# Queries and keys turned by VectorE in 32x32 blocks instead of by TensorE, with a fourth buffer for the activation tiles

## The chip, the cores and the metric

One core of one Trainium2 chip runs the whole program. The metric is the device time of one execution in microseconds, from the first to the last instruction and what the launch adds around them; smaller is better. TensorE, VectorE, ScalarE, GpSimd and SyncE run side by side, each in its own program order, and wait for one another by semaphores. SyncE issues every transfer of this kernel; sixteen DMA engines carry them out.

## The reference

Chunked attention with a few memory keys in front, then two feed-forward networks, all in float32:

```python
# q, k, v: 4 x 8 heads x 768 x 64; mem_k, mem_v: 4 x 8 x 8 x 64
for c in range(S // 32):                       # chunks of 32 queries
    l, r = max(0, 32 * c - 16), min(S, 32 * c + 32 + 8)
    k_full = concatenate([mem_k, k[:, :, l:r]], axis=2)
    v_full = concatenate([mem_v, v[:, :, l:r]], axis=2)
    a = softmax(q[:, :, 32 * c:32 * c + 32] @ k_full.T / 8)
    out[:, :, 32 * c:32 * c + 32] = a @ v_full
x = out as 3072 tokens x 512
x = (s * relu(x @ w_in) ** 2 + b) @ w_out      # 512 -> 2048 -> 512
x = (silu(x @ w_gate) * (x @ w_val)) @ w_out2  # 512 -> 1536 -> 512
```

## The kernel before

Attention is worked off in 24 groups of 128 queries (`GQ`), six to a batch, all eight heads at once. A group needs its queries and keys with the head dimension on the partitions, because TensorE contracts over partitions. `load_tokens` brings them in row by row (a token on each partition, 256-byte pieces, one for each head); `stage_queries` and `stage_keys` turn them on TensorE by products with the identity into the PSUM tiles `psQ` and `psK`, and `stage_queries_copy` and `stage_keys_copy` (lines L228 and L230) copy them to `qt` and `kt` in SBUF. `kt` holds for each of the group's four chunks the 8 memory keys and a window of 56 keys. Then come the scores (`psS`), the softmax, its turning (`psA`), the product with the values (`psV`) and the turning of the result (`psO`) into the tiles `xhi` and `xlo`. Where the values of one group and the scores of the next fall on one place, `stage_both` merges them in one block, `psB`.

The first network runs over 8 blocks of 384 tokens (three groups each) and 16 slices of its 2048 hidden columns. A step is twelve products into `hp` (the up product) and twelve into `acc` (the down product); between them ScalarE and VectorE make relu, square, bias and the split of the result into a rounded part `ghi` and a rest `glo`. `r` is the tile of this work, three buffers in the pool `gp`, and the copies `y` of finished blocks take their buffers from the same three. Weights come in raw as `raw_first` (1 MB for each slice) and are split into such pairs by ScalarE and VectorE (`split`, lines L774 to L838). The second network has three passes over the same tokens, with a scheme of seven products per block.

The order of all this is written by the class `Plan`: each piece of work is a task with an engine, a planned length, the tasks it depends on, and rings of buffers that it takes and gives. TensorE's order is that in which tasks are added; for the other engines and for SyncE's queue a list scheduler picks the next ready task by the longest way to the end. `START` is the order on TensorE at the beginning, when the first groups are worked off before and between the first steps; `VISITS` says at which half step of a block each stage of the later groups stands; `LOADS` fixes the order of the first transfers; `MOVED` names tasks that take the second of two possible engines. Groups 0 to 5 (`EARLY`) keep their queries and keys in slots of the weight pool, and only groups 6 to 23 use the tiles `q`, `ka` and `kb`.

```python
        t = plan.add(PE, 0.44, lambda: stage_queries(g, early), [qk], take=["acc2"] if early else ["a"])
```

Of the kernel before, what the change touches and what calls it, by code (L numbers as in the profile page):

```python
# [10 lines left out]
F32 = mybir.dt.float32  # L11
# [8 lines left out]
CHUNK, LEFT, RIGHT = 32, 16, 8  # L20
GQ = 128
# [6 lines left out]


START = (  # L30
    "Q0 T0 S0 Q1 T1 A0 V0 S1 Q2 A1 T2 X0 S2 V1 A2 X1 V2 X2 Q3 T3 U S3 Q4 U A3 D T4 U S4 D V3 "
    "U A4 X3 Q5 D V4 U T5 X4 D U S5 D A5 V5 X5 D U "
)

VISITS = {
# [6 lines left out]
}  # L42

LOADS = (
    "W0 K0 W2 K1 V0 W1 K2 V1 W4 V2 K3 W3 K4 V3 W6 W5 K5 V4 W9 W8 V5 W7 W10 "
)

MOVED = (
# [10 lines left out]
)  # L59


# [84 lines left out]
def attention_and_two_mlps(  # L146
# [52 lines left out]
    LENT = 3  # L199
    EARLY = 2 * GPB  # L200

    const = ctx.enter_context(tc.tile_pool(name="const", bufs=1))
    wp = ctx.enter_context(tc.tile_pool(name="wp", bufs=SLOTS))
    xp = ctx.enter_context(tc.tile_pool(name="xp", bufs=2))
    gp = ctx.enter_context(tc.tile_pool(name="gp", bufs=3))
    stp = ctx.enter_context(tc.tile_pool(name="stp", bufs=2))
    dram = ctx.enter_context(tc.tile_pool(name="dram", bufs=1, space=DRAM))
    ps_acc = ctx.enter_context(tc.tile_pool(name="ps_acc", bufs=1, space=PSUM))
# [17 lines left out]
    def copy(engine, out, in_):  # L226
        if engine == "ACT":
            nc.scalar.activation(out=out, in_=in_, func=AF.Copy)  # L228
        else:
            nc.vector.tensor_copy(out, in_)  # L230
# [58 lines left out]
    def load_tokens(g):  # L289

        b, gi = divmod(g, GB)
        s0 = gi * GQ
        if g < EARLY:
            t = wp.tile([P, 4, H * D], F32, tag="w", name=f"qk{g}")
            tq, ka, kb, sc = (t[:, i] for i in range(4))
        else:
            tq, ka, kb = (ld.tile([P, H * D], F32, tag=n, name=f"{n}{g}") for n in ("q", "ka", "kb"))
            sc = None
        every = slice(0, H)
        a, z = s0 - LEFT, s0 + GQ + RIGHT  # L300
        left, over, n = max(0, -a), max(0, z - S), HALF - NMEM
        rows(ka, mem_k, b, every, 0, NMEM)
        if left:
            rows(ka[NMEM:], k, b, every, 0, left)
        rows(ka[NMEM + left:], k, b, every, a + left, n - left)
        rows(tq, q, b, every, s0, GQ)
        rows(kb, k, b, every, a + n, HALF - over)
        if over:
            rows(kb[HALF - over:], k, b, every, S - over, over)
        loaded.setdefault(g, {}).update(q=tq, ka=ka, kb=kb, sc=sc)  # L310

    def load_values(g):

        b, gi = divmod(g, GB)
        s0 = gi * GQ
        n = g % 2
        if n not in v_bufs:
            v_bufs[n] = ld.tile([P, NC, NP, D], F32, tag=f"v{n}", name=f"v{n}")
        tv = v_bufs[n]
        for e in range(2):  # L320
            p0 = e * KC
            if gi < 2:
                mem = tv[p0:p0 + NMEM]
                nc.sync.dma_start(out=mem[:, 0], in_=mem_v[b, e:H:2].rearrange("h s d -> s h d"))
                for c in range(1, NC):
                    nc.gpsimd.tensor_copy(mem[:, c], mem[:, 0])
            for c in range(NC):
                a = s0 + c * CHUNK - LEFT
                left, over = max(0, -a), max(0, a + WIN - S)
                for row, first, n in (  # L330
                    (0, 0, left), (left, a + left, WIN - left - over), (WIN - over, S - over, over)
                ):
                    if n:
                        r0 = p0 + NMEM + row
                        nc.sync.dma_start(
                            out=tv[r0:r0 + n, c],
                            in_=v[b, e:H:2, first:first + n, :].rearrange("h s d -> s h d"),
                        )
        loaded.setdefault(g, {})["v"] = tv
# [65 lines left out]

    def scores_to(g):
        if "sc" not in staged[g]:
            sc = loaded[g]["sc"]
            if sc is None:
                sc = ap_.tile([P, H * KC], F32, tag="sc", name=f"sc{g}")  # L410
            staged[g]["sc"] = sc.rearrange("p (j e s) -> p j e s", j=NP, e=2)
        return staged[g]["sc"]
# [322 lines left out]
    def second_store(h, s, i):  # L735
# [7 lines left out]
    plan = Plan(  # L743
        dict(w=SLOTS - LENT, wt=SLOTS - 2, fly=2),
        dict(
            sc=LENT, f=2, own=1, qk=1, v=2, kt=1, qt=1, at=1, on=1, x=2, r=3, ghi=2, glo=2, acc01=1,
            acc2=1, acc3=1, a=2, h=2, yq=1, so=1, z=5, a1=1, a2=1, a3=1, v1=2, v2=1,
        ),
    )
# [3 lines left out]
    def either(name, lengths, emit, *args, **kwargs):  # L753

        engine = list(lengths)[name in moved]
        return plan.add(engine, lengths[engine], lambda: emit(engine), *args, **kwargs)

    issues = {}

    def transfer(deps, emit, n, kilobytes, get=(), take=(), give=(), rate=380.0, name=None):  # L760

        issue = issues[name] = plan.add(SP, 0.45 * n, emit, deps, [*get, "fly"], take=take)
        return plan.add(MOVE, kilobytes / rate, None, [issue], put=["fly"], lag=1.8, give=give)
# [97 lines left out]
    at_ = {}  # L861

    def plan_queries(g, early):
        qk = transfer(
            [], lambda: load_tokens(g), 4, 590, take=["sc"] if g < EARLY else ["qk"], rate=180.0, name=f"K{g}"
        )
        vv = transfer([], lambda: load_values(g), 8, 460, take=["v"], rate=180.0, name=f"V{g}")
        at_[g] = {"v": vv, "qk": qk}
        t = plan.add(PE, 0.44, lambda: stage_queries(g, early), [qk], take=["acc2"] if early else ["a"])
        at_[g]["qt"] = either(  # L870
            f"q{g}", {ACT: 0.50, DVE: 0.60}, lambda e: stage_queries_copy(e, g), [t], take=["qt"],
            give=["acc2"] if early else ["a"],
        )

    def plan_keys(g, early):
        t = plan.add(
            PE, 0.55, lambda: stage_keys(g, early), [at_[g]["qk"]], take=["acc01"] if early else ["a", "a"],
            give=[] if g < EARLY else ["qk"],
        )
        for i in range(2):  # L880
            t = either(
                f"k{g}_{i}", {ACT: 0.45, DVE: 0.54}, lambda e, i=i: stage_keys_copy(e, g, i, False), [t],
                take=["kt"] if i == 0 else (),
            )
            t = either(
                f"m{g}_{i}", {ACT: 0.26, DVE: 0.20}, lambda e, i=i: stage_keys_copy(e, g, i, True), [t],
                give=[] if early else ["a"],
            )
        if early:
            plan.rings["acc01"].append(t)  # L890
        at_[g]["t"] = at_[g]["qt"], t
# [66 lines left out]

    def plan_w1(m):
        if m not in split1:  # L960
            landed = transfer([], lambda: load_w1(m), 2, 1024, ["w", "w"], name=f"W{m}")
            split1[m] = split(landed, raw1, m, lambda: wp, f"first{m}", w1)

    def plan_up1(t, m):
# [287 lines left out]
```

## Time and profile before

| | us |
|---|---|
| median of three runs (1245.95 to 1248.83) | 1245.95 |
| the profiled execution, its own time | 1246.5 |
| its span, first to last instruction | 1244.7 |
| TensorE busy | 1204.2 |
| VectorE busy | 737.4 |
| ScalarE busy | 531.9 |
| GpSimd busy | 26.5 |

The busy times come from the page's first part. They are sums over the program, and the stages differ, so a change is read from the stretch in which it lies. The span is 1.8 us shorter than the execution's own time, which also has what lies around the first and last instruction.

### The profile page before, as it was taken

To read this page: it belongs to the slowest core of one execution; us is meant where nothing else is said; L and a number is where in the kernel's file an instruction comes from. 1 tells how busy PE (TensorE), PEld (TensorE's weight loads), DVE (VectorE), ACT (ScalarE), POOL (GpSimd) and SP (SyncE) were. 2 spreads that over 40 slices of the span, in tenths; PEclk is the share of its full clock that TensorE was granted. 3 is DMA by queue.
4 is the path that set the end of the run, shared out by engine and by line. 5 is a ranking of instruction groups with operands and counts; after the bars stand their busy time and mean duration, and the time that the engine had idled before them with its cause. 6 is when DMAs were issued, how large, how long until landed. Compare 5 with 4: busy or idle time off the path is not lost.

```text
span 1244.7 us, 25671 instructions
## 1 busy us (share of the span) xinstructions
PE 1204.2 (97%) x10512; PEld 1145.3 (92%) x10512; DVE 737.4 (59%) x1435; ACT 531.9 (43%) x1100; POOL 26.5 (2%) x54
## 2 busy tenths in 40 slices
PE   4788999999999999999999999999999999999998
PEld 3678999999999999999999999999999999999997
DVE  6889874444344343443579876668964448744444
ACT  4454532434333333333358554445543335433332
POOL 2011000000000000000000000000000000000000
PEclk9998999999999999999999999999999999999999
DMA  8864242212222122230273555567755558545532
GB/s 190 219 182 166 88 112 43 60 36 61 55 50 60 36 61 54 50 92 4 99 248 119 162 187 186 186 234 283 249 193 186 185 186 312 195 187 187 187 119 94
DMA packets 168014, 174.31 MB, mean 140 GB/s; under 512 B 108376, under 2 KB 139608, under 8 KB 166360
## 3 DMA queue, kind: packets, MB, share of 16 engines
q1 hardware_dynamic: 167896, 172.66, 43.2%
q8 instruction: 83, 1.36, 0.4%
q14 instruction: 35, 0.29, 0.1%
HBM read 124.65 MB, written 47.97 MB: 139 GB/s over the span
## 4 chain that ended last, share of the span: by engine, by line
PE 90%; DMA 4%; SPq 2%; DVE 2%; issue 1%; ACT 1%; POOL 0%; DVEq 0%; ACTq 0%; POOLq 0%
PE acc L494 7%; PE hp L494 7%; PE acc L495 7%; PE acc L496 7%; PE hp L496 7%; PE hp L495 7%; PE chain_a L494 5%; PE chain_a L495 5%; PE chain_a L496 5%; PE oacc L495 5%; PE oacc L494 5%; PE oacc L496 5%; PE chain_b L495 4%; PE chain_b L496 4%; PE chain_b L494 4%; DMA raw_first<-in_moe_w_out_dram 2%
## 5 line engine op out<-in xcount | busy, mean ns | idle before, releaser
L494 PE MATMUL acc<-ghi,w_first 128*128 128x384 f32 x512 | 177.7, 347 | 4.2 <-DVE ghi L547 3.9
L494 PE MATMUL hp<-xhi,w_first 128*128 128x384 f32 x512 | 176.5, 345 | 0.6 <-ACT xhi L228 0.6
L495 PE MATMUL acc<-glo,w_first 128*128 128x384 f32 x512 | 172.6, 337 | 0.2 <-DVE glo L556 0.2
L496 PE MATMUL acc<-ghi,w_first 128*128 128x384 f32 x512 | 172.6, 337 | 0.0
L495 PE MATMUL hp<-xlo,w_first 128*128 128x384 f32 x512 | 171.9, 336 | 0.4 <-DVE xlo L487 0.4
L496 PE MATMUL hp<-xhi,w_first 128*128 128x384 f32 x512 | 171.9, 336 | 0.0
L682 ACT ACTIVATE kept<-chain_a 128x256 f32<-128x256 f32 x216 | 82.9, 384 | 159.5 <-PE chain_a L496 131.9
L534 DVE SCALAR_TENSOR_TENSOR r<-r,s_sb 128x384 f32<-128x384 f32 x89 | 55.0, 618 | 145.8 <-ACT r L523 145.6
L523 ACT ACTIVATE r<-hp 128x384 f32<-128x384 f32 x107 | 52.7, 492 | 204.2 <-PE hp L496 204.1
L494 PE MATMUL oacc<-w_down,ghi 128*128 128x512 f32 x288 | 114.2, 396 | 0.1
L495 PE MATMUL oacc<-w_down,ghi 128*128 128x512 f32 x288 | 114.2, 397 | 0.0
L496 PE MATMUL oacc<-w_down,glo 128*128 128x512 f32 x288 | 112.2, 389 | 0.0
L494 PEld LDWEIGHTS acc<-ghi,w_first 128*128 128x128 f32 x512 | 96.8, 189 | 6.1 <-issue 4.2
L494 PEld LDWEIGHTS hp<-xhi,w_first 128*128 128x128 f32 x512 | 96.6, 189 | 2.4 <-ACT xhi L228 0.9
L495 PEld LDWEIGHTS acc<-glo,w_first 128*128 128x128 f32 x512 | 96.8, 189 | 0.8 <-DVE glo L556 0.8
L495 PEld LDWEIGHTS hp<-xlo,w_first 128*128 128x128 f32 x512 | 96.7, 189 | 0.7 <-DVE xlo L487 0.7
L496 PEld LDWEIGHTS acc<-ghi,w_first 128*128 128x128 f32 x512 | 96.8, 189 | 0.0
L496 PEld LDWEIGHTS hp<-xhi,w_first 128*128 128x128 f32 x512 | 96.3, 188 | 0.0
L699 DVE TENSOR_TENSOR v<-v,g 128x256 f32<-128x256 f32 x144 | 60.9, 423 | 56.0 <-ACT g L695 54.2
L687 DVE TENSOR_TENSOR v<-chain_b,kept 128x256 f32<-128x256 f32 x144 | 60.8, 423 | 37.7 <-PE chain_b L496 25.5
L707 DVE TENSOR_TENSOR glo<-v,ghi 128x256 fp32r<-128x256 f32 x144 | 60.6, 421 | 37.1 <-ACT ghi L228 37.0
L494 PE MATMUL chain_a<-y,hi_up 128*128 128x256 f32 x288 | 81.4, 283 | 0.6 <-ACT kept L682 0.5
(139 smaller groups left out, 2740.7 us busy)
## 6 DMA issues: line engine op xcount, KB each, us to landing
y<-ops_dram SPq DMA_DIRECT2D x48, 512.0 KB
ops_dram<-y SPq DMA_DIRECT2D x24, 512.0 KB
sum_dram<-o SPq DMA_DIRECT2D x48, 256.0 KB
o<-sum_dram SPq DMA_DIRECT2D x12, 1024.0 KB
v<-in_v_dram SPq DMA_DIRECT2D x176, 56.0 KB
yhi<-ops_dram_hi SPq DMA_DIRECT2D x12, 768.0 KB
ylo<-ops_dram_lo SPq DMA_DIRECT2D x12, 768.0 KB
raw_first<-in_moe_w_in_dram SPq DMA_DIRECT2D x16, 512.0 KB
```

The costliest lines, as they stand in the source:

```text
L494: nc.tensor.matmul(o, whi, xhi, start=first, stop=False, skip_group_check=onto)
L495: nc.tensor.matmul(o, whi, xlo, start=False, stop=False, skip_group_check=onto)
L496: nc.tensor.matmul(o, wlo, xhi, start=False, stop=last, skip_group_check=onto)
L523: nc.scalar.activation(out=r, in_=hp, func=AF.Relu)
L534: nc.vector.scalar_tensor_tensor(out=r, in0=r, scalar=s_sb[:, 0:1], in1=r, op0=ALU.mult, op1=ALU.mult)
L682: nc.scalar.activation(out=t, in_=st2[n]["A"], func=AF.Copy)
L687: nc.vector.tensor_tensor(out=t, in0=st2[n]["B"], in1=st2[n].pop(f"a{i}"), op=ALU.add)
L699: nc.vector.tensor_tensor(out=v, in0=v, in1=g, op=ALU.mult)
L707: nc.vector.tensor_tensor(out=lo, in0=st2[n].pop(f"v{half + 1}"), in1=st2[n][f"hi{half}"].bitcast(F32), op=ALU.subtract)
```

## The change

For groups 6 to 23 (7 to 24, counted from one) TensorE no longer turns queries and keys. The loads bring each quarter of the partitions (a `QUAD` of 32) in with 32 tokens on the partitions and 32 of the head's 64 numbers in a row, so that a piece is 128 bytes. VectorE then turns each 32x32 block with one instruction for the queries (`turn_queries`, 128x512) and one for the keys and memory keys (`turn_keys`, 128x640, into the new tile `kT`); `spread_keys` copies the four windows from `kT` to `kt` on ScalarE (128x896) and the memory keys on either engine (128x256). The tasks for `psQ` and `psK` and their copies are gone for these groups. The input tiles `qin` and `kin` are one buffer each, and so are `kT`, `kt` and `qt`. The pool of `r` and `y` has four buffers instead of three. The tables `START`, `VISITS`, `LOADS` and `MOVED` are replaced, and the planner counts the first network's weight loads at a lower rate.

```diff
 START = (
-    "Q0 T0 S0 Q1 T1 A0 V0 S1 Q2 A1 T2 X0 S2 V1 A2 X1 V2 X2 Q3 T3 U S3 Q4 U A3 D T4 U S4 D V3 "
+    "Q0 T0 S0 Q1 A0 V0 T1 S1 X0 Q2 T2 A1 S2 V1 X1 A2 V2 Q3 T3 X2 S3 U U Q4 D T4 U A3 S4 D V3 "
...
-    gp = ctx.enter_context(tc.tile_pool(name="gp", bufs=3))
+    gp = ctx.enter_context(tc.tile_pool(name="gp", bufs=4))
...
+    def load_quadrant(g, a, part):
...
+        e, half = divmod(a, 2)
+        ds = slice(half * QUAD, (half + 1) * QUAD)
+        qin, kin = loaded[g]["q"][a * QUAD:(a + 1) * QUAD], kept_in["k"][a * QUAD:(a + 1) * QUAD]
...
+        for j in (2 * part - 2, 2 * part - 1):
+            h = 2 * j + e
+            first = at + QUAD - NMEM
+            nc.sync.dma_start(
+                out=kin[:, j, 1:1 + whole],
+                in_=k[b, h, first:first + whole * QUAD, ds].rearrange("(n t) i -> t n i", t=QUAD),
+            )
+            nc.sync.dma_start(
+                out=qin[:, j], in_=q[b, h, s0:s0 + GQ, ds].rearrange("(n t) i -> t n i", t=QUAD)
+            )
+
+    def turn_queries(g):
+        staged[g] = {"qt": ap_.tile([P, NP, GQ], F32, tag="qt", name=f"qt{g}")}
+        nc.vector.transpose(
+            out=staged[g]["qt"].rearrange("p j s -> p (j s)"), in_=loaded[g]["q"].rearrange("p j n i -> p (j n i)")
+        )
...
     def plan_queries(g, early):
+        vv = None
+        if g >= EARLY:
+            qk = None
+            for a in range(12):
+                qk = transfer(
+                    [issues[f"K{g}_{a - 1}"]] if a else [], lambda a=a: load_quadrant(g, *divmod(a, 3)), 4 if a % 3 else 1,
+                    64 if a % 3 else 14, take=["qk"] if a == 0 else (), rate=100.0, name=f"K{g}_{a}",
+                )
...
+            t = plan.add(DVE, 0.60, lambda: turn_queries(g), [qk], take=["qt"])
+            at_[g] = {"v": vv, "qt": t}
+            t = plan.add(DVE, 0.72, lambda: turn_keys(g), [t], take=["kT"], give=["qk"])
+            t = plan.add(ACT, 0.82, lambda: spread_keys(ACT, g, False), [t], take=["kt"])
+            t = either(f"m{g}", {ACT: 0.26, DVE: 0.20}, lambda e: spread_keys(e, g, True), [t], give=["kT"])
...
     def plan_keys(g, early):
+        if g >= EARLY:
+            return
```

The tables decide where the new instructions stand. The first place is SyncE's queue in the middle of the first network, where one group's query and key loads end and the next group's begin. Before, a group is four or five issues (`ka`, `q`, `kb`) beside eight or ten of values (`v`):

```order
L335 DMA v_190<-in_v_dram 56x4x64 x8
L284 DMA ka_2612<-in_mem_k_dram 8x8x64
L284 DMA ka_2612<-in_k_dram 72x8x64
L284 DMA q_2611<-in_q_dram 128x8x64
L284 DMA kb_2613<-in_k_dram 80x8x64
L579 DMA y_dram_88<-y 128x384 x4
```

Now the same place reads:

```order
L346 DMA kin<-in_k_dram 32x4x32
L350 DMA qin_2554<-in_q_dram 32x4x32
L401 DMA v_167<-in_v_dram 56x4x64 x8
L327 DMA kin<-in_k_dram 24x4x32 x2
L327 DMA kin<-in_k_dram 8x4x32
L346 DMA kin<-in_k_dram 32x3x32
L350 DMA qin_2859<-in_q_dram 32x4x32
```

The pairs of `kin` and `qin` repeat 16 times in a group, with one to three smaller issues at each quarter: 36 issues for a group inside a batch, 44 for the first and the last of a batch. The value loads stand behind all of them, and the stores of `y` between two of them.

The second place is VectorE behind a merged block of values and scores. Before:

```order
L415 TENSOR_TENSOR sc_3974<-psB_0_3879,mx_3971 128x4x64
L415 TENSOR_TENSOR sc_3974<-psB_1_3880,mx_3971 128x4x64
L534 SCALAR_TENSOR_TENSOR r<-r,s_sb 128x384
L487 TENSOR_TENSOR xlo_3988<-psO_3977,xhi_3987 128x4x128
L456 TENSOR_REDUCE rc_4004<-sc_3974 128x8
L459 TENSOR_SCALAR rc_4004<-rc_4004 128x8
L460 RECIPROCAL rc_4004<-rc_4004 128x8
L556 SCALAR_TENSOR_TENSOR glo<-r,b_sb,ghi 128x384
```

Now, five steps after the turning of the group before:

```order
L600 SCALAR_TENSOR_TENSOR r<-r,s_sb 128x384
L522 TENSOR_REDUCE rc_4472<-sc_4445 128x8
L525 TENSOR_SCALAR rc_4472<-rc_4472 128x8
L526 RECIPROCAL rc_4472<-rc_4472 128x8
L622 SCALAR_TENSOR_TENSOR glo<-r,b_sb,ghi 128x384
L356 STREAM_TRANSPOSE qt_4493<-qin_4202 128x512
L362 STREAM_TRANSPOSE kT_4500<-kin 128x640
L600 SCALAR_TENSOR_TENSOR r<-r,s_sb 128x384
L553 TENSOR_TENSOR xlo_4200<-psO_4495,xhi_4199 128x4x128
```

The two turnings stand between the `glo` of one step and the `r` of the next; whatever they wait for holds every instruction behind them.

## Rows read from the trace of the kernel before

**Rows 1.** The page: the span, and the chain that ended last by engine.
```profile
span 1244.7 us, 25671 instructions
...
PE 90%; DMA 4%; SPq 2%; DVE 2%; issue 1%; ACT 1%; POOL 0%; DVEq 0%; ACTq 0%; POOLq 0%
```

**Rows 2.** Two stretches: busy time (instructions) by engine, TensorE clock, DMA share, GB/s.
```profile
0.00:124.00 124.00, 89.36 (x1167) 79.24 (x1168) 100.31 (x166) 57.37 (x92) 16.77 (x30) 0.97 0.71 190
124.00:600.00 476.00, 476.00 (x5014) 466.58 (x5016) 222.26 (x445) 178.97 (x353) 9.75 (x24) 1.00 0.23 56
```

**Rows 3.** Order of time on TensorE: start, duration, instruction; two transposes between products.
```profile
304.40 0.34 PE L495 MATMUL hp<-xlo,w_first 128*128 128x384 f32 x1
304.57 0.34 PE L496 MATMUL hp<-xhi,w_first 128*128 128x384 f32 x1
304.75 0.60 PE L349 MATMUL psQ<-ident,q 128*128 128x128 f32 x4
...
305.36 0.34 PE L495 MATMUL acc<-glo,w_first 128*128 128x384 f32 x1
```

**Rows 4.** The same view nine microseconds on, around one group's key transposes.
```profile
313.34 0.34 PE L496 MATMUL hp<-xhi,w_first 128*128 128x384 f32 x1
313.51 0.23 PE L360 MATMUL psK<-ident,ka 80*128 80x80 f32 x1
...
314.29 0.34 PE L495 MATMUL acc<-glo,w_first 128*128 128x384 f32 x1
```

**Rows 5.** TensorE, 124 to 600 us, by line and shape: count | busy us, mean ns.
```profile
L349 PE MATMUL psQ<-ident,q 128*128 128x128 f32 x72 | 10.8, 272 | 0.0
```

**Rows 6.** Order of time on TensorE: a merged block of values and scores.
```profile
289.46 0.34 PE L496 MATMUL hp<-xhi,w_first 128*128 128x384 f32 x1
...
291.50 0.34 PE L495 MATMUL acc<-glo,w_first 128*128 128x384 f32 x1
```

**Rows 7.** The same view: a block of scores alone.
```profile
134.94 0.34 PE L496 MATMUL hp<-xhi,w_first 128*128 128x384 f32 x1
...
136.28 0.34 PE L495 MATMUL acc<-glo,w_first 128*128 128x384 f32 x1
```

**Rows 8.** Order of time on SyncE's queue: one group's loads as issued.
```profile
469.73 0.30 SPq L284 DMA_DIRECT2D ka<-in_mem_k_dram  x1
470.08 0.33 SPq L284 DMA_DIRECT2D ka<-in_k_dram  x1
...
471.01 0.52 SPq L284 DMA_DIRECT2D kb<-in_k_dram  x1
472.62 3.62 SPq L335 DMA_DIRECT2D v<-in_v_dram  x8
```

**Rows 9.** The same view: the slowest eight value loads after the start.
```profile
161.40 6.12 SPq L335 DMA_DIRECT2D v<-in_v_dram  x8
```

**Rows 10.** SyncE's queue, line L284: durations of one issue, ns, min/median/max.
```profile
L284 SPq DMA_DIRECT2D ka<-in_k_dram x21: 300/322/408, 67.0 to 547.8; - x21
L284 SPq DMA_DIRECT2D kb<-in_k_dram x21: 483/524/727, 68.3 to 549.2; - x21
L284 SPq DMA_DIRECT2D ka<-in_mem_k_dram x18: 272/286/330, 66.6 to 547.4; - x18
```

**Rows 11.** SyncE's queue, line L335: the value loads, the same columns.
```profile
L335 SPq DMA_DIRECT2D v<-in_v_dram x208: 311/368/1831, 12.2 to 555.1; - x104
```

**Rows 12.** The chain that ended last: one value load, from issue to landing.
```profile
92.07 1.66 DMA v<-in_v_dram
```

**Rows 13.** One stretch, columns as in rows 2, while query, key and value loads move.
```profile
314.80:318.50 3.70, 3.70 (x141) 3.36 (x141) 1.27 (x4) 1.01 (x3) 0.00 (x0) 1.00 0.85 168
```

**Rows 14.** VectorE, 124 to 600 us, by line and shape.
```profile
L487 DVE TENSOR_TENSOR xlo<-psO,xhi 128x512 fp32r<-128x512 f32 x17 | 11.8, 692 | 6.2 <-ACT xhi L228 6.2
...
L230 DVE COPY y<-acc 128x384 f32<-128x384 f32 x12 | 6.5, 552 | 2.7 <-DMA y_dram<-y 2.6
```

**Rows 15.** Order of time on TensorE: the longest wait behind the first half block.
```profile
102.09 0.66 PE L494 MATMUL acc<-ghi,w_first 128*128 128x384 f32 x1 [3.94 <-DVE ghi L547]
```

More of the change, by code (lines that the diff above doesn't have):

```diff
@@ L30 @@
 START = (
-    "Q0 T0 S0 Q1 T1 A0 V0 S1 Q2 A1 T2 X0 S2 V1 A2 X1 V2 X2 Q3 T3 U S3 Q4 U A3 D T4 U S4 D V3 "
-    "U A4 X3 Q5 D V4 U T5 X4 D U S5 D A5 V5 X5 D U "
+    "Q0 T0 S0 Q1 A0 V0 T1 S1 X0 Q2 T2 A1 S2 V1 X1 A2 V2 Q3 T3 X2 S3 U U Q4 D T4 U A3 S4 D V3 "
+    "U D A4 Q5 T5 X3 U V4 X4 D U S5 D A5 D V5 X5 U "
 )
 VISITS = {
[6 rows of a table removed]
[6 rows of a table added]
 }
 LOADS = (
-    "W0 K0 W2 K1 V0 W1 K2 V1 W4 V2 K3 W3 K4 V3 W6 W5 K5 V4 W9 W8 V5 W7 W10 "
+    "W0 K0 W1 V0 K1 K2 W2 V1 W4 V2 K3 W3 V3 K4 W6 K5 W5 V4 W8 V5 W7 W10 W9 "
 )
 MOVED = (
[10 rows of a table removed]
[11 rows of a table added]
 )
@@ L292, in load_tokens @@
         s0 = gi * GQ
[L293 to L298, printed above, removed]
+        t = wp.tile([P, 4, H * D], F32, tag="w", name=f"qk{g}")
+        tq, ka, kb, sc = (t[:, i] for i in range(4))
         every = slice(0, H)
@@ L310, in load_tokens, with block @@
         loaded.setdefault(g, {}).update(q=tq, ka=ka, kb=kb, sc=sc)
+    QUAD = P // 4
+    KB = (NMEM + SPAN) // QUAD
+    kept_in = {}
+    def load_quadrant(g, a, part):
+        b, gi = divmod(g, GB)
+        s0 = gi * GQ
+        if a == 0 and part == 0:
+            if "k" not in kept_in:
+                kept_in["k"] = ld.tile([P, NP, KB, QUAD], F32, tag="kin", name="kin")
+            loaded.setdefault(g, {})["q"] = ld.tile([P, NP, GQ // QUAD, QUAD], F32, tag="qin", name=f"qin{g}")
+        e, half = divmod(a, 2)
+        ds = slice(half * QUAD, (half + 1) * QUAD)
+        qin, kin = loaded[g]["q"][a * QUAD:(a + 1) * QUAD], kept_in["k"][a * QUAD:(a + 1) * QUAD]
+        def block(n, t, first, count):
+            if count:
+                nc.sync.dma_start(
+                    out=kin[t:t + count, :, n], in_=k[b, e:H:2, first:first + count, ds].rearrange("j t i -> t j i")
+                )
+        at = s0 - LEFT
+        left, over = max(0, -at), max(0, at + SPAN - S)
+        whole = KB - 1 - (over > 0)
+        if part == 0:
+            if gi == 0:
+                nc.sync.dma_start(out=kin[0:NMEM, :, 0], in_=mem_k[b, e:H:2, :, ds].rearrange("j t i -> t j i"))
+            block(0, NMEM, 0, left)
+            block(0, NMEM + left, at + left, QUAD - NMEM - left)
+            if over:
+                block(KB - 1, 0, S - QUAD + over, QUAD - over)
+                block(KB - 1, QUAD - over, S - over, over)
+            return
[6 more added lines that the diff above has]
+            )
+            nc.sync.dma_start(
+                out=qin[:, j], in_=q[b, h, s0:s0 + GQ, ds].rearrange("(n t) i -> t n i", t=QUAD)
+            )
@@ new lines, in turn_queries, with turn_keys @@
+    def turn_queries(g):
[3 more added lines that the diff above has]
+        )
+    def turn_keys(g):
+        staged[g]["kT"] = t = ap_.tile([P, NP, KB * QUAD], F32, tag="kT", name=f"kT{g}")
+        nc.vector.transpose(
+            out=t.rearrange("p j s -> p (j s)"), in_=kept_in["k"].rearrange("p j n i -> p (j n i)")
+        )
@@ new lines, in spread_keys @@
+    def spread_keys(engine, g, mem):
+        kT = staged[g]["kT"]
+        if mem:
+            copy(
+                engine, staged[g]["kt"][:, :, :, 0:NMEM],
+                kT[:, :, 0:NMEM].unsqueeze(2).to_broadcast([P, NP, NC, NMEM]),
+            )
+            return
+        staged[g]["kt"] = kt = ap_.tile([P, NP, NC, KC], F32, tag="kt", name=f"kt{g}")
+        w = kT[:, :, NMEM:KC]
+        copy(engine, kt[:, :, :, NMEM:], bass.AP(tensor=w.tensor, offset=w.offset, ap=[w.ap[0], w.ap[1], [CHUNK, NC], [1, WIN]]))
@@ L407, in scores_to @@
         if "sc" not in staged[g]:
-            sc = loaded[g]["sc"]
+            sc = loaded[g].get("sc")
             if sc is None:
@@ L745, in attention_and_two_mlps @@
         dict(
-            sc=LENT, f=2, own=1, qk=1, v=2, kt=1, qt=1, at=1, on=1, x=2, r=3, ghi=2, glo=2, acc01=1,
+            sc=LENT, f=2, own=1, qk=1, v=2, kT=1, kt=1, qt=1, at=1, on=1, x=2, r=4, ghi=2, glo=2, acc01=1,
             acc2=1, acc3=1, a=2, h=2, yq=1, so=1, z=5, a1=1, a2=1, a3=1, v1=2, v2=1,
@@ L863, in plan_queries @@
     def plan_queries(g, early):
+        vv = None
[5 more added lines that the diff above has]
+                    64 if a % 3 else 14, take=["qk"] if a == 0 else (), rate=100.0, name=f"K{g}_{a}",
+                )
+                if a == 5:
+                    vv = transfer([], lambda: load_values(g), 8, 460, take=["v"], rate=180.0, name=f"V{g}")
+            t = plan.add(DVE, 0.60, lambda: turn_queries(g), [qk], take=["qt"])
[3 more added lines that the diff above has]
+            t = either(f"m{g}", {ACT: 0.26, DVE: 0.20}, lambda e: spread_keys(e, g, True), [t], give=["kT"])
+            at_[g]["t"] = at_[g]["qt"], t
+            return
         qk = transfer(
-            [], lambda: load_tokens(g), 4, 590, take=["sc"] if g < EARLY else ["qk"], rate=180.0, name=f"K{g}"
+            [], lambda: load_tokens(g), 4, 590, take=["sc"], rate=180.0, name=f"K{g}"
         )
@@ L875, in plan_keys @@
     def plan_keys(g, early):
+        if g >= EARLY:
+            return
         t = plan.add(
             PE, 0.55, lambda: stage_keys(g, early), [at_[g]["qk"]], take=["acc01"] if early else ["a", "a"],
-            give=[] if g < EARLY else ["qk"],
         )
@@ L960, in plan_w1 @@
         if m not in split1:
-            landed = transfer([], lambda: load_w1(m), 2, 1024, ["w", "w"], name=f"W{m}")
+            landed = transfer([], lambda: load_w1(m), 2, 1024, ["w", "w"], rate=300.0, name=f"W{m}")
             split1[m] = split(landed, raw1, m, lambda: wp, f"first{m}", w1)
```

33 rows, old and new, of tables (MOVED, VISITS) are left out of this document.

## The prediction

> **What bounds the kernel now.** I read the page first, for the chain that ended last, and then the busy times by stretch. The chain runs over TensorE for 90% of the span [rows 1]. By stretch the program has two parts that this change can touch. From 124 to 600 us TensorE is busy for 476.00 of 476.00 us at the full clock, while VectorE is busy for 222.26 of them, ScalarE for 178.97, and the DMA engines for a share of 0.23 [rows 2]. There, a microsecond less on TensorE is a microsecond less in all, as long as nothing else comes late. Before 124 us TensorE stands idle for 124.00 - 89.36 = 34.6 us [rows 2]; that stretch goes by transfers and by VectorE (100.31 us busy), and TensorE's work is not its price. The second network behind 600 us is not edited apart from the fourth buffer.
>
> **What is removed.** In order of time the starts of TensorE's products give the price of a transposing block, since products overlap and busy times would count the overlap twice. One product of the network follows the last after about 0.1735 us: from 305.36 to 313.34 there are 46 starts [rows 3, 4]. Around the query transposes, the product before starts at 304.57 and the second one behind at 305.36; less two steps that is 0.79 - 0.35 = 0.44 us [rows 3]. Around the key transposes it is 313.34 to 314.29, less two steps: 0.95 - 0.35 = 0.60 us [rows 4]. There are 72 query transposes from 124 to 600 us, four to a group [rows 5]: all 18 groups that change lie in the stretch where TensorE never waits. So 18 x 1.04 = 18.8 us of TensorE go. The new order has 15 merged blocks of values and scores where there were 16. A merged block costs 291.50 - 289.46 - 0.35 = 1.69 us [rows 6], scores alone 136.28 - 134.94 - 0.35 = 0.99 us [rows 7]; values alone have as many products and I take 0.99 for them too. One pair unmerged costs 1.98 - 1.69 = 0.3 us. Net: 18.5 us.
>
> **What is added, and what hides it.** VectorE gets two turnings a group. None is in this trace. Its 128x512 operation takes 0.692 us [rows 14]; 640 numbers at that rate are 0.87 us. Nothing says that a turning is dearer or cheaper by number, so I take 1.5 us a group, with half of it and twice of it as bounds (0.8 and 3.1 us). ScalarE loses the copies from `psQ` and `psK` and gets one from `kT`, about even. VectorE has 53% of the stretch free, ScalarE 62% [rows 2], so the sum is hidden; what isn't hidden by a sum is the order, and that is a rival below. If the cover were gone, 18 x 1.5 = 27 us would show.
>
> SyncE gets the most new work. A group was four or five issues for queries and keys; now it is 36, or 44 at the ends of a batch, on average (4 x 36 + 2 x 44) / 6 = 38.7. None of that size is timed as such; the neighbours are 0.286 us for the 64 pieces of the memory keys, 0.322 for key rows, 0.368 for a value load, and 0.524 for the dearest, `kb` [rows 10, 11]. Between two issues 0.05 us pass (469.73 + 0.30 to 470.08) [rows 8]. A new issue has 96 or 128 pieces, between the memory keys and a value load; I take 0.33 + 0.05 = 0.38 us and keep 0.34 and 0.57 as ends. Eight value loads take 3.62 us [rows 8], at worst 6.12 [rows 9]; most of that difference is single issues that hang for a microsecond (the longest took 1.831 us [rows 11]), so I allow 2 us a group for such hangs in the longer list. A group's turn of the queue is 38.7 x 0.38 + 4.5 (values) + 0.6 (its third of four stores) + 2 = 21.8 us.
>
> What it may take follows from TensorE: a block of 384 tokens is 16 steps of 24 products and three groups' merged blocks, `psA` and `psO` (as long as a query transpose, with as many products): 16 x 24 x 0.1735 + 3 x (1.69 + 0.44 + 0.44) = 74.3 us, so 24.8 us a group. 21.8 fits. The tighter loop is the one through the single buffers: `turn_keys` frees `kin`, then the next group's loads are issued, land, and must be there when VectorE comes to the next turning, five steps later, 5 x 24 x 0.1735 + 2.57 = 23.4 us. Loads of 36 issues need 13.7 us, of 44 issues 16.7, plus at most 2 for hangs and 1.66 for landing [rows 12]: 17 to 20.4 us. The value loads stand behind them in the queue, and stores of `y` inside. It closes with 3 to 6 us to spare; spare time ends at 0.48 us an issue by the first sum ((24.8 - 7.1) / 38.7 = 0.46) and near the same by the second.
>
> The pieces: while query, key and value loads moved, 168 GB/s for 3.70 us are 2428 pieces of 256 bytes, and 0.85 of sixteen engines for 3.70 us are 50.3 us, so 20.7 ns a piece [rows 13]. A group's 4608 pieces of 128 bytes at that full price are 95 us of one engine, 6.0 us of all sixteen; at half price 3.0. Either fits into 24.8 us beside a share of 0.23.
> The Trainium skill speaks against this part: "DMA: Bandwidth & Descriptors", in Rules for kernel authors, wants many small transfers gathered into one and says that under 64 KB one pays mostly overhead; an issue here is 12 to 16 KB. If the overhead were paid one transfer after another, the loop could not close. The trace disagrees as far as overlap goes: value loads of 56 KB are issued every 0.45 us while one takes 1.66 us to land.
>
> **The fourth buffer.** From 124 to 600 us it is VectorE that waits for a store of `y`, 2.6 us in all [rows 14], while TensorE does not wait. Worth nothing there.
>
> **The start.** The new tables change what precedes the first uninterrupted steps. The longest wait behind the first half block is 3.94 us for `ghi`, at 102.09 [rows 15], which stands on VectorE behind two weight splits. In the new queue one pair of weight loads fewer (1 MB, 5.5 us at the 190 GB/s of that stretch [rows 2]) and fewer loads of later groups precede the weights of those splits; on the other hand VectorE does eleven more operations by then, at 0.5 to 0.7 us some 6 us, against 24 us of idle time in that stretch (124.00 - 100.31). I take 2 us of gain, with ends at 6 gained and 6 lost.
>
> **Sum.** The profiled execution took 1246.5 us (span 1244.7), half a microsecond over the median of three. 1246.5 - 18.5 - 2 = 1226.
>
> **The rivals.**
> (a) *The queue doesn't keep up.* If an issue takes what `kb` takes, 0.524 + 0.05 = 0.57 us, a group's turn is 38.7 x 0.57 + 7.1 = 29.2 us, 4.4 more than TensorE leaves. The turning waits, and because VectorE works in order, `r` and `glo` of the network wait behind it, and TensorE behind them: 17 x 4.4 = 75 us, less 20: about 1300, slower. It decides from 0.46 us an issue. For it: `kb` and the hangs; against it: the issues with few pieces are all under 0.37 us. If small transfers landed one after another (38.7 x 1.66 = 64 us a group) it would be far worse; I hold that part for nearly excluded. Chance 0.10.
> (b) *VectorE's order costs.* The two turnings and one longer ScalarE copy stand among the ten operations behind each merged block. `glo` of a step must be ready about 4.2 us after that of the last. If each group costs TensorE 0.5 to 1 us, 9 to 18 us of the gain go: 1235 to 1244. Against it: 53% free, and TensorE waited nowhere in that stretch though the same crowd (without the turnings) stands there. Chance 0.10.
> (c) *The start loses* instead of gaining, up to 6 us, because some 80 issues of the first two changed groups (30 us of the queue) share it with the last weights: up to 1234. Chance 0.12.
> (d) *Nothing comes of it:* gain and loss within 0.3%. Chance 0.04.
>
> **How the numbers follow.** My forecast, transposes gone and loops closed with a start between 5 us better and 2 us worse, has 0.64: 1223 to 1230, and 1226 as its middle. The range must hold eight in ten: with (c) and most of (b), and the lower end of the start, it is 1219 to 1240. Faster by over 0.3% (3.7 us, about what a measurement here can tell from no change) are the forecast, (c), and most of (b): 0.85. Same: (d) and the end of (b), 0.05. Slower: (a), 0.10.
>
> **What would show it.** Right: from about 120 us to the end of the first network TensorE busy without a gap, that stretch some 18 us shorter, no `psQ` and `psK` there; turnings near 0.6 to 0.9 us; issues of `kin` and `qin` of 0.30 to 0.36 us and hardly any idle time of VectorE before a turning that ends with a DMA. Wrong: TensorE waiting for `glo`, `ghi` or `kt`, with VectorE idle before a turning until `kin` or `qin` landed (a), or busy without a break (b). The forecast is most open to the time of one small issue, which no row shows, and to the start.

## The result and the profile after

| | before | after |
|---|---|---|
| median, us | 1246.74 (4 runs, 1245.95 to 1248.83) | 1235.88 (4 runs, 1233.53 to 1236.99) |
| profiled execution, us | 1246.5 | 1235.41 |
| ratio | | 0.9908 [0.9888, 0.9928] |

The change is worth 10.9 us. The direction was right and the time lies in the range, but 9.9 us above the forecast and outside the forecast's own 1223 to 1230. The profile shows in which of its terms.

The page of the changed kernel first: span, and the chain that ended last by engine.

```profile
span 1233.6 us, 25831 instructions
...
PE 79%; SPq 9%; DMA 6%; DVE 3%; issue 2%; ACT 1%; DVEq 0%; ACTq 0%
```

Against [rows 1] the chain has lost eleven points on TensorE, and SyncE's queue has gone from 2% to 9%. By stretch, columns as in [rows 2]:

```profile
0.00:124.00 124.00, 89.07 (x1156) 79.17 (x1157) 103.85 (x175) 53.30 (x81) 9.56 (x24) 0.90 0.72 179
124.00:600.00 476.00, 473.06 (x4883) 462.44 (x4882) 259.64 (x507) 162.50 (x289) 13.20 (x30) 1.00 0.27 59
```

TensorE now stands idle for 2.9 us from 124 to 600 us, where it had been busy throughout. Two waits in the order of time on TensorE carry most of that:

```profile
274.56 0.44 PE L560 MATMUL acc<-ghi,w_first 128*128 128x384 f32 x1 [1.63 <-DVE ghi L231]
...
422.42 0.44 PE L561 MATMUL acc<-glo,w_first 128*128 128x384 f32 x1 [0.64 <-DVE glo L622]
```

The first of these waits costs more than its length. By stretch, just behind it:

```profile
276.00:278.00 2.00, 2.00 (x8) 2.00 (x7) 0.55 (x1) 1.35 (x3) 0.55 (x2) 0.50 0.38 76
...
280.00:282.00 2.00, 2.00 (x15) 1.97 (x14) 0.93 (x2) 0.00 (x0) 0.00 (x0) 1.00 0.24 38
```

From 276 to 278 us TensorE's granted clock is 0.50, the lower level of 1.2 GHz, and products start 0.32 us apart, against 0.17 at 1.00. The twelve products from 274.56 on take 3.83 us (to 278.39), where the same twelve take 2.08 in the run lean below, which has no such wait and a clock of 1.00 there. Of the 1.75 us more, some 0.5 lie in the first three starts (274.56, 275.15, 275.43), the rest in the lower clock. The engine counts as busy for nearly all of it, so it is not in the 2.9 us.

VectorE in order of time just ahead of the two waits:

```profile
247.06 0.72 DVE L356 STREAM_TRANSPOSE qt<-qin 128x512 f32<-128x512 f32 x1 [2.25 <-DMA qin<-in_q_dram]
...
272.23 0.71 DVE L356 STREAM_TRANSPOSE qt<-qin 128x512 f32<-128x512 f32 x1 [3.33 <-DMA v<-in_mem_v_dram]
272.86 0.80 DVE L362 STREAM_TRANSPOSE kT<-kin 128x640 f32<-128x640 f32 x1
273.59 0.65 DVE L553 TENSOR_TENSOR xlo<-psO,xhi 128x512 fp32r<-128x512 f32 x1
274.16 0.34 DVE L231 CAST ghi<-r 128x384 fp32r<-128x384 f32 x1
...
421.15 0.71 DVE L356 STREAM_TRANSPOSE qt<-qin 128x512 f32<-128x512 f32 x1 [1.93 <-DMA v<-in_mem_v_dram]
```

At 272.23 VectorE has waited 3.33 us in front of the query turning; behind it stand the key turning, `xlo` and the `ghi` for which TensorE waits until 274.56. The turning reads no values: `v` is only the last transfer to land in that piece of queue, which says that the whole queue is late. Of the 17 turnings in this stretch only the three shown wait for over 0.35 us; eight wait for nothing. The three belong to groups 12, 13 and 19, counted from one: the last of a batch and two first of a batch, all with 44 issues. (Groups 18 and 24 have as many and wait for 0.17 us: from the first of their issues to the moment when VectorE was ready they had 24.5 and 26.0 us, group 12 had 23.3.) By line, from 124 to 600 us:

```profile
L362 DVE STREAM_TRANSPOSE kT<-kin 128x640 f32<-128x640 f32 x17 | 13.9, 818 | 0.0
...
L356 DVE STREAM_TRANSPOSE qt<-qin 128x512 f32<-128x512 f32 x17 | 12.0, 708 | 8.7 <-DMA v<-in_mem_v_dram 5.6 <-DMA qin<-in_q_dram 2.2 <-DMA v<-in_v_dram 0.7
L231 DVE COPY y<-acc 128x384 f32<-128x384 f32 x11 | 5.9, 553 | 0.3
```

The turnings cost 0.71 + 0.82 = 1.53 us a group, as forecast, and waited 8.7 us in all. The wait for stores of `y` [rows 14] has gone. And SyncE's queue at the first group of a batch, one quarter of the partitions from its memory keys to those of the next quarter:

```profile
250.02 0.27 SPq L336 DMA_DIRECT2D kin<-in_mem_k_dram  x1
250.34 0.68 SPq L327 DMA_DIRECT2D kin<-in_k_dram  x2
251.06 0.32 SPq L346 DMA_DIRECT2D kin<-in_k_dram  x1
251.42 0.43 SPq L350 DMA_DIRECT2D qin<-in_q_dram  x1
251.89 0.42 SPq L346 DMA_DIRECT2D kin<-in_k_dram  x1
252.36 0.43 SPq L350 DMA_DIRECT2D qin<-in_q_dram  x1
...
254.74 0.33 SPq L336 DMA_DIRECT2D kin<-in_mem_k_dram  x1
```

The pairs follow one another every 0.475 us (251.42 to 251.89, 252.36), not every 0.38; the eleven issues of the quarter take 254.74 - 250.02 = 4.72 us. A quarter inside a batch lacks the memory keys and one short piece, about 0.7 us, so 4.0.

The lateness begins one group earlier, at group 12, whose loads fill the queue between these rows:

```profile
218.77 1.79 SPq L401 DMA_DIRECT2D v<-in_v_dram  x4
221.50 1.07 SPq L327 DMA_DIRECT2D kin<-in_k_dram  x3
...
224.44 1.97 SPq L645 DMA_DIRECT2D y_dram<-y  x4
...
245.71 4.21 SPq L401 DMA_DIRECT2D v<-in_v_dram  x10
```

The queue is free from 220.56 on and the first issue follows at 221.50, when the key turning of group 11 (from 220.63) is done with `kin`. So here it is not a backlog but the loop through the single buffer that is too long: 44 issues, four stores and two hung issues (1.56 and 1.70 us) last until 245.61, 24.1 us. Group 13 then starts late, at 250.02, because group 12's values stand ahead of its loads.

How far one kernel is ahead of another is read by the starts of TensorE's products, counted in order of time; a half step of the first network is twelve of them. Where half steps 22 and 216 (before: 121.56 and 591.05 us) begin, against the kernel before (plus is later), in each profiled execution, one for each kernel:

| kernel | 22: the start, us | 216, us | gained between |
|---|---|---|---|
| changed | +1.3 | -11.4 | 12.7 |
| changed, run again | +2.3 | -10.9 | 13.2 |
| lean | +2.1 | -15.7 | 17.8 |
| queries_gpsimd | -0.1 | -18.5 | 18.5 |
| no_queries | +2.3 | -15.1 | 17.4 |
| lean_queries_gpsimd | +1.9 | -16.4 | 18.4 |
| eight_more | +4.9 | +41.2 | -36.4 |
| lean_turn_twice | +4.5 | -3.7 | 8.3 |
| lean_queries_gpsimd_turn_twice | +3.4 | -8.0 | 11.4 |
| lean_three_buffers | +6.1 | -11.5 | 17.6 |
| start_old | +5.3 | -1.6 | 6.9 |
| before_new_start | +3.5 | +4.8 | -1.3 |
| before_four | -1.3 | +0.4 | -1.7 |

The forecast was -2 us for the start and 18.5 gained behind it. The changed kernel shows +1.3 and 12.7: 3.3 and 5.8 us short. Theory 1 says that the 5.8 are SyncE's price for an issue, theory 2 that the 3.3 are the new order of the start. The rivals: VectorE's order is too full, or the small transfers themselves are late.

### The profile page after: what moved, and what is told of

The parts are those of the page before. It is cut to its first block, busy times and chain, and to the rows that moved or that the text cites. A ratio compares the mean times of both kernels' runs of the same rounds, so it can differ in the third digit from the quotient of the medians.

```text
span 1233.6 us, 25831 instructions
## 1 busy us (share of the span) xinstructions
PE 1189.7 (96%) x10296; PEld 1129.8 (92%) x10296; DVE 773.4 (63%) x1496; ACT 506.3 (41%) x1018; POOL 22.8 (2%) x54
## 4 chain that ended last, share of the span: by engine, by line
PE 79%; SPq 9%; DMA 6%; DVE 3%; issue 2%; ACT 1%; DVEq 0%; ACTq 0%
PE chain_a L560 6%; PE chain_a L561 6%; PE chain_a L562 6%; PE oacc L561 5%; PE oacc L560 5%; PE oacc L562 5%; PE acc L560 5%; PE acc L561 5%; PE acc L562 5%; PE hp L560 5%; PE hp L562 5%; PE hp L561 5%; PE chain_b L561 4%; PE chain_b L562 4%; PE chain_b L560 4%; SPq L350 3%
## 5 line engine op out<-in xcount | busy, mean ns | idle before, releaser
L589 ACT ACTIVATE r<-hp 128x384 f32<-128x384 f32 x96 | 47.1, 491 | 186.1 <-PE hp L562 179.1
```

Source lines behind the costliest of these rows:

```text
L589: nc.scalar.activation(out=r, in_=hp, func=AF.Relu)
```

## The experiments

**Fewer issues (lean).** Rows that the mask covers anyway aren't loaded again, behind the first use:

```diff
-            block(0, NMEM, 0, left)
+            block(0, NMEM, 0, left if g == EARLY else 0)
...
-                block(KB - 1, QUAD - over, S - over, over)
+                block(KB - 1, QUAD - over, S - over, 0 if g > GB else over)
...
-                    if n:
+                    if n and (row == left or g <= GB):
```

> The changed kernel without the loads of rows that the mask covers anyway (keys and values ahead of a batch's first row and behind its last): the first and last group of a batch issue 40 query and key loads instead of 44, and 8 value loads instead of 10. Theory 1 (an issue of SyncE costs 0.475 us, and only the groups with 44 issues come late): VectorE's waits before its turnings at 247, 272 and 421 us (2.25, 3.33 and 1.93 us) fall by at least 1.9 us each, TensorE's waits of 1.63 us for ghi at 274.6 and 0.64 us for glo at 422.4 vanish, and the time falls by 2.5 to 5 us, to 1231 to 1233.5. Rival 1 (VectorE's order is too full): the waits of TensorE stay and the time is within 1 us of 1235.9. Rival 2 (transfers, not issues, are late): the fewer issues carry 3% less, and the waits shrink by less than 0.5 us.

Measured: 1228.38 us (5 runs), ratio 0.9866 [0.9843, 0.9889]. By the medians, which were not taken side by side, that is 7.5 us under the changed kernel; by the ratios, each to the kernel before measured beside it, 0.0042 or 5.2 us, just over the 2.5 to 5 expected. From 124 to 600 us, by stretch and by VectorE's line:

```profile
124.00:600.00 476.00, 475.44 (x4909) 465.93 (x4910) 264.35 (x516) 164.50 (x293) 14.09 (x30) 1.00 0.27 60
...
L356 DVE STREAM_TRANSPOSE qt<-qin 128x512 f32<-128x512 f32 x17 | 12.0, 707 | 1.3 <-DMA qin<-in_q_dram 0.6 <-DMA v<-in_v_dram 0.5
```

The waits before the turnings fall from 8.7 to 1.3 us, TensorE waits nowhere for over 0.2 us, and 5.1 us more are gained in this stretch, as the ratios have it. Rivals 1 and 2 fall for these 5.1 us. In order of time the changed kernel loses 1.8 of them to lean in the wait of 274.56, 2.1 in the two half steps behind it, mostly by the lower clock, and 0.9 at the wait of 422.42.

**Queries on another queue (queries_gpsimd).**

```diff
-            nc.sync.dma_start(
+            nc.gpsimd.dma_start(
                 out=qin[:, j], in_=q[b, h, s0:s0 + GQ, ds].rearrange("(n t) i -> t n i", t=QUAD)
```

> The changed kernel with the sixteen query loads of each changed group issued by GpSimd instead of SyncE; nothing else is edited. Theory 1: a group's turn of SyncE's queue falls by 16 x 0.475 = 7.6 us, no turning waits for keys any more, and the time falls by 3 to 6 us to 1230 to 1233, if GpSimd issues one in under 1 us (16 must go by in 23 us). Rival 1 (VectorE's order): no change, 1235 to 1237. Rival 2 (the transfers themselves): the same pieces move, so no change either. If GpSimd needs over 1.4 us an issue, its queue is late in place of SyncE's, and the time is 1240 or more.

Measured: 1231.79 us (5 runs), 0.9878 [0.9856, 0.9899]. The issues on GpSimd, ns, and TensorE's stretch:

```profile
L350 POOL DMA_DIRECT2D qin<-in_q_dram x288: 548/548/1001, 28.8 to 519.9; - x144
...
124.00:600.00 476.00, 475.58 (x4913) 466.19 (x4912) 264.95 (x517) 163.75 (x293) 154.21 (x286) 1.00 0.25 59
```

The same pieces, the same turnings, and all 18.5 us are there. (The profiled execution is the fastest of the five, 1228.67 us.) So it was the issuing, not the moving. The Trainium skill ("Trainium Kernel Development and Optimization", Key Constraints) says that transfers issued from SyncE, ScalarE and GpSimd run on the same sixteen engines and that spreading them only saves issue time; that is just what this run saved.

**No query loads (no_queries).** The `dma_start` of `qin` is under `if g == EARLY`, and the first changed group's tile serves all others.

> Leaves out the query loads of all changed groups but the first, which uses wrong queries; sixteen issues and 2048 pieces fewer a group, all else as in the changed kernel. Theory 1: it bounds what the late queue costs: 3 to 6 us under the changed kernel, 1230 to 1233, and TensorE waits nowhere from 124 to 600 us. Rival 1 (VectorE's order): 1235 to 1237, since the two turnings stay. Rival 2 (the price of moving small pieces slows all other transfers too): more than 6 us, under 1229, with a good part of it before 124 us.

Measured: 1230.46 us (4 runs), 0.9865 [0.9836, 0.9894]; 17.4 us gained between the half steps, no wait over 0.3 us on TensorE behind 124. Not below the two kernels that keep the loads: nothing else of the loads costs time there. It shows no saving before 124 us either.

**Eight issues more (eight_more).**

```diff
+            split = 2 if j < 2 else 1
+            for n0 in range(0, 4, 4 // split):
+                ns, first = slice(n0, n0 + 4 // split), s0 + n0 * QUAD
...
```

> The changed kernel with eight of a group's sixteen query loads split in two: the same pieces, eight issues more a group (46.7 on average). Theory 1 (the queue's time is issues times 0.475 us): a group's turn is 46.7 x 0.475 + 7.1 = 29.3 us against 24.8 us that TensorE leaves, 4.5 us late in each of 17 groups: about 1228 + 76 = 1304 us, and VectorE waits for qin or kin before nearly every turning. If a half-sized issue costs only 0.33 + 0.05 us, it is 2.3 us more a group instead of 3.8: near 1275. Rival 1 (VectorE's order) and rival 2 (the transfers): no more bytes and no more work, so 1234 to 1240.

Measured: 1290.11 us (3 runs), 1.0342 [1.0301, 1.0382]: far over the 1234 to 1240 of the rivals, and 14 us under the 1304 of theory 1, which counts every issue at 0.475 us. VectorE's query turnings from 124 to 600 us, and a piece of SyncE's queue in order of time with the two halves of one query load merged in a row:

```profile
L360 DVE STREAM_TRANSPOSE qt<-qin 128x512 f32<-128x512 f32 x17 | 12.1, 710 | 59.4 <-DMA qin<-in_q_dram 35.0 <-DMA v<-in_mem_v_dram 18.0 <-DMA v<-in_v_dram 6.4
...
330.25 0.43 SPq L346 DMA_DIRECT2D kin<-in_k_dram  x1
330.72 0.90 SPq L353 DMA_DIRECT2D qin<-in_q_dram  x2
331.67 0.43 SPq L346 DMA_DIRECT2D kin<-in_k_dram  x1
```

Rival (a) of the prediction, produced at will: 59.4 us of waits before the turnings. Two half-sized loads take 0.90 us with one gap, 0.43 each, as much as a whole one: the price goes by issues. With the measured quarters, and the prediction's 7.1 us for values, stores and hung issues: 4 x 4.0 + 7.1 = 23.1 us for a group inside a batch, 4 x 4.72 + 7.1 = 26.0 for an end group; eight issues more at 0.475 make 26.9 and 29.8, on average 27.9, 3.1 over TensorE's 24.8. That is 53 us in 17 groups; the table shows 18.4 + 36.4 = 54.8.

**Both edits (lean_queries_gpsimd), and the changed kernel beside it (after_again).**

> The edits of lean and queries_gpsimd together: SyncE issues 24 small loads for an end group of a batch and 20 for another, GpSimd sixteen at 0.55 us. Theory 1 (each of the two edits alone already takes the lateness of the queue away): no more than 1 us under queries_gpsimd alone in the stretch from 124 to 600 us, where 18.5 us of TensorE's time is all there is to win; 1227 to 1231. Rival (issues still cost something in the other groups too): 1225 or less.

> The changed kernel itself, beside the run lean_queries_gpsimd on the same chip, so that the two can be told apart: 1234 to 1237 us as before, 4 us or more over the other. If it is within 2 us of the other, what lean and queries_gpsimd seemed to win was a difference between chips.

Measured: 1229.92 us (5 runs), 0.9871 [0.9853, 0.9889], with 18.4 us gained between the half steps; the changed kernel again 1234.73 (5 runs), 0.9911 [0.9897, 0.9925], with a wait of 1.93 us for `ghi` at the same place. Either edit alone takes the lateness away, and there is no more to get. These two kernels ran on one chip: the slowest run of the one took 1232.20 us, the fastest of the other 1234.45. (The interval of lean ends at 0.9889; that of the changed kernel begins at 0.9897 here and at 0.9888 in the first measurement.)

**Turnings done twice (lean_turn_twice, lean_queries_gpsimd_turn_twice).**

```diff
-        nc.vector.transpose(
+        for _ in range(2):
+          nc.vector.transpose(
...
```

> The kernel of the run lean with each of the two turnings done twice by VectorE: 18 x 1.52 = 27 us more work there, no other edit. Theory (the turnings are hidden, only their inputs were late): 1228 to 1232 us, TensorE busy for over 475 of 476 us from 124 to 600. Rival (VectorE's order costs TensorE something at each turning): 0.5 to 1 us a group, 1237 to 1246.

> The kernel of the run lean_queries_gpsimd with both turnings done twice, so that the loads have room and only VectorE's time is doubled. In lean the second turning cost 9.6 us from 124 to 600 us. Theory (most of that was the queue again, since doubled turnings free kin 1.5 us later a group): from 124 to 600 us less than 3 us are lost against lean_queries_gpsimd, 1230 to 1233 in all. Rival (VectorE's order: behind a merged block there is no room for 3 us): 6 to 10 us are lost there, 1235 or more, with VectorE not waiting for any load before a turning.

Measured: 1242.36 us (10 runs), 0.9967 [0.9952, 0.9982], and 1240.03 (5 runs), 0.9953 [0.9934, 0.9971]. Between the half steps 17.8 - 8.3 = 9.5 us are lost to lean, and 18.4 - 11.4 = 7.0 with the queries on GpSimd. Both theories are missed, and both times fall where the rival has them. I had expected the queue to explain most of it, and it explains 2.5. In the second of the two, VectorE in order of time ahead of TensorE's longest wait behind 124 us, 1.47 us for the `ghi` of 153.18:

```profile
147.73 1.72 DVE L364 STREAM_TRANSPOSE kT<-kin 128x640 f32<-128x640 f32 x2
149.37 0.65 DVE L848 TENSOR_SCALAR t_first<-t_first 128x1024 f32<-128x1024 f32 x1
150.05 0.69 DVE L852 TENSOR_SCALAR t_first<-t_first 128x1024 uint32<-128x1024 uint32 x1
150.78 1.23 DVE L857 SCALAR_TENSOR_TENSOR raw_first<-raw_first,t_first 128x1024 uint32<-128x1024 uint32 x1
152.04 1.23 DVE L864 SCALAR_TENSOR_TENSOR raw_first<-raw_first 128x1024 uint32<-128x1024 uint32 x1
153.18 0.35 DVE L231 CAST ghi<-r 128x384 fp32r<-128x384 f32 x1
```

No idle time in any row: VectorE is simply full there, with the last weight split between the turning and `ghi`. Later places, in either run, lose 0.2 to 1.4 us each. So the turnings are hidden at 1.5 us a group and not at 3: rival (b) is wrong for this change and right for twice its work.

**Three buffers (lean_three_buffers, before_four).** `bufs` of `gp` and the ring `r`, 4 to 3 in lean, 3 to 4 in the kernel before.

> The kernel of the run lean with three buffers for r and y, as before the change. Theory (the fourth buffer is worth nothing): 1227 to 1230 us; VectorE waits some 2.6 us for stores of y, and TensorE does not wait. Rival (the fourth buffer is what lets VectorE run ahead past the turnings): TensorE waits for glo or ghi at block ends, 3 us or more, 1232 or more.

> The kernel before with four buffers for r and y, nothing else edited: this part of the change alone. In lean the fourth buffer was worth 4 us ahead of 124 us and nothing behind. Theory (it helps only where splits of the weights stand ahead of ghi on VectorE, in the start of either kernel): 2 to 5 us less, 1242 to 1245. Rival (the start's table was chosen for four buffers, so that lean lost where its own order didn't fit three): no change, 1245 to 1249, or slower.

Measured: 1235.55 us (4 runs), 0.9906 [0.9876, 0.9935], some 7 us over lean, where the theory had 1227 to 1230; and 1245.75 (10 runs), 0.9994 [0.9982, 1.0006], nothing. (By the ratios it is 5.0 us over lean; the medians come from two chips.) Behind 124 us three buffers gain as much as four (17.6 and 17.8), though VectorE waits 2.5 us for stores of `y`. The loss lies ahead of it, at one place. TensorE, and then VectorE's rows ahead of that wait, with three buffers:

```profile
117.18 0.44 PE L560 MATMUL acc<-ghi,w_first 128*128 128x384 f32 x1 [2.54 <-DVE ghi L231]
...
113.43 0.55 DVE L591 TENSOR_SCALAR r<-hp 128x384 f32<-128x384 f32 x1
113.90 1.22 DVE L862 SCALAR_TENSOR_TENSOR raw_first<-raw_first 128x1024 uint32<-128x1024 uint32 x1
115.03 1.22 DVE L904 TENSOR_TENSOR w_first<-raw_first,w_first 128x1024 fp32r<-128x1024 f32 x1
116.17 0.68 DVE L231 CAST w_first<-raw_first 128x1024 fp32r<-128x1024 f32 x1
116.77 0.35 DVE L231 CAST ghi<-r 128x384 fp32r<-128x384 f32 x1
```

The same two in lean:

```profile
110.41 0.52 DVE L591 TENSOR_SCALAR r<-hp 128x384 f32<-128x384 f32 x1
...
114.04 0.55 DVE L231 CAST ghi<-r 128x384 fp32r<-128x384 f32 x1
```

With four buffers the planner puts `r` ahead of one weight split; with three it comes 3 us later, and `ghi` stands behind a second. Of the 4.0 us by which this kernel is behind lean at half step 22, the wait is 2.5; the rest comes behind it, where the granted clock is 0.64 from 118 to 122 us, against 1.00 in lean. It is the order of VectorE in the start, not a buffer that comes free late on the chip. In the kernel before, with its own start, there is no such place: the theory expected 2 to 5 us there and was wrong.

**The order of the start (start_old, before_new_start).** `START` and `LOADS` exchanged between the two kernels, nothing else.

> The changed kernel with the start order and the order of the first loads of the kernel before (START and LOADS alone). Theory 2 (the new order of the start costs some 4 us against the old one, 1.5 to 2 lost where 2 were forecast as won): first product at 46 instead of 51 us, and the time falls by 2 to 5 us to 1231 to 1234. Rival (the start loses because the first changed groups' 88 issues stand in the queue with the last weights, whatever the order): first product earlier, but what was won is lost again by 124 us, and the time is 1235 or more.

> The kernel before with the changed kernel's START and LOADS, queries and keys still turned by TensorE: the order of the start alone. Theory (the order belongs to the small loads, it makes room for them and wins nothing by itself): 1244 to 1250 us, with the first product near 50 us and no more than 2 us less by 124 us. Rival (the order of the start is better by itself, and the run start_old lost 11 us for that reason): 1235 to 1241 us.

Measured: 1247.45 us (10 runs), 1.0006 [0.999, 1.0022], and 1250.46 (10 runs), 1.0024 [1.0006, 1.0042]. Theory 2 falls: with the old order the changed kernel loses 11.6 us, and the new order alone makes the old kernel slower, by some 3 us. In start_old the largest loss ahead of half step 22 is a wait for values, TensorE's row first, then SyncE's:

```profile
90.84 0.39 PE L511 MATMUL psV<-v,at 64*32 64x64 f32 x2 [7.09 <-DMA v<-in_v_dram]
...
82.59 9.08 SPq L401 DMA_DIRECT2D v<-in_v_dram  x10
```

In the kernel before, the ten value loads at this place are issued from 71.10; here 29 small loads, from 66.03 to 80.43, stand ahead of them, where the kernel before has five. Later in start_old, SyncE's queue as the last weights are issued, and TensorE where they are needed:

```profile
160.61 0.43 SPq L346 DMA_DIRECT2D kin<-in_k_dram  x1
161.08 0.43 SPq L350 DMA_DIRECT2D qin<-in_q_dram  x1
161.61 0.39 SPq L240 DMA_DIRECT2D raw_first<-in_moe_w_in_dram  x1
...
175.06 0.69 PE L560 MATMUL hp<-xhi,w_first 128*128 128x384 f32 x1 [4.14 <-DVE w_first L231]
```

The last weight load comes at 161.61 us, between the small loads, where the kernel before had it at 139.09 and the changed kernel at 153.43. In start_old 27 small loads, from 148.16 on, stand directly ahead of it. Behind the wait of 4.14 us the granted clock is 0.50 from 176 to 180 us. So the small loads delay the weights, as rival (c) said, and the new tables are what keeps that from showing more. start_old differs from the kernel before in `VISITS`, `MOVED` and the planner's rate for weights too; no run exchanges one of these alone.

## Why the prediction was right in part

- **What is removed: right.** 18.5 us were forecast, 18.4 and 18.5 are gained where the queue is relieved.
- **The queue: the mechanism was named, its price was too low, and the average group was asked instead of the worst.** The step that failed is "a new issue has 96 or 128 pieces, between the memory keys and a value load; I take 0.33 + 0.05". In pairs it is 0.475 start to start, 0.44 on average over a group, and it does not follow the pieces. The break-even of 0.46 was that of the average group; 44 x 0.38 + 7.1 = 23.8 us would still have fitted, 4 x 4.72 + 7.1 = 26.0 does not. (The 0.48 ahead of that quotient is a slip; the 2 us for hung issues were about right, 30 of the 638 small ones from 124 to 545 us took over 0.6 us, 1.5 us a group in excess of the median.) The tighter loop, through the single buffers, was to close "with 3 to 6 us to spare": at group 12 it asks 24.1 us for the issues where 16.7 and 2 were counted, and VectorE waits. The last group of a batch and the first of the next follow each other: VectorE waits 2.25 us at the one and 3.33 at the other, and by these sums the queue recovers at 24.8 - 23.1 = 1.7 us a group. Price: 17.8 - 12.7 = 5.1 us, shown by lean; some 2 of them lie behind a wait, mostly in products at the lower clock, for which the prediction has no term. That is rival (a) in a mild form at its edge.
- **VectorE: right**, 1.53 us a group for 1.5, hidden. But "53% free" was not the reason to trust: at 3 us a group, the upper bound that I also called hidden, 7 us of TensorE go.
- **The fourth buffer: right behind 124 us, not priced ahead of it,** where under the new order three buffers lose 4 us at half step 22. By itself, in the kernel before, it is worth nothing.
- **The start: wrong sign.** 2 us gained were forecast; +1.3 and +2.3 are measured. I took the fewer weight loads ahead of the splits as a gain and gave the small loads' delay a chance of only 0.12. Changing the order by itself costs 3.5 us in the profiled execution. Which wait of the new start carries the rest stays open: the changed kernel, its repeat and the four with fewer issues on SyncE differ by up to 2.4 us at half step 22 (-0.1 to +2.3), with no rule by the number of issues.
- **Sum:** 1246.5 - 12.7 + 1.3, and 0.3 from there to the end, is the 1235.4 of the profiled execution. That the time lies in the range is in part luck: (c) was given times up to 1234 and (b) 1235 to 1244, so that 1235.9 stands in the part held for (b), which did not come; a mild (a) and a mild (c) happen to add up to as much.

Lean beats both kernels, at 1228.4 us; GpSimd's idle queue does about as much without leaving out a load.

## What to carry to other kernels

Where many small loads replace a few, price the queue that issues them by the count, for the worst group as well as for the average, and ask what stands behind the instruction that waits for them on its in-order engine. A margin of one or two microseconds a round is decided by an issue's 0.1 us; loading less at the edges, or giving a third of the issues to an idle engine, is a cheap way out. An engine with half its time free may still have no room for 1.5 us more at the place that counts: look at the row ahead of the wait, not at the share.

## What the runs showed of the hardware

- SyncE's issue of a small load is 0.32 us for the first of a row and 0.42 to 0.43 behind it, with 0.045 between, whole or halved. GpSimd's is 0.548 at the median and 1.0 at most.
- Single issues on SyncE's queue take up to 1.96 us (line L350, changed kernel), against a median of 0.430.
- From 40 to 50 us TensorE's granted clock was 0.50, the lower level of 1.2 GHz, in the changed kernel, with TensorE busy for 6.0 of ten us in each of the two stretches ahead of it; in the kernel before, busy for 6.7 and 6.6 there, it stayed at 1.00. The first product of the network starts 4.8 us later there, and all but 0.5 of it is won back by 109 us. That is not what makes the first product late: in lean_three_buffers and before_new_start the granted clock was 1.00 from 20 to 60 us, and the first product starts 4.7 and 4.3 us later than in the kernel before all the same.
- In or behind a long wait of TensorE in the first network the granted clock was 0.50 for some microseconds: behind 1.63 us of waiting at 274.56 in the changed kernel, 1.93 at 275.36 in its repeat, 2.54 at 117.18 in lean_three_buffers, 4.14 at 175.06 in start_old. A product then starts 0.32 us after the last, and 0.17 at 1.00. No run changes the clock alone, so that the wait brings it on is not shown by itself.
